# Retention attention and a GELU MLP on one core: q of chunks 3 to 5 transposed by VectorE instead of TensorE, attention given due times, one last copy

## The chip, the cores and the metric

One core of one Trainium2 chip. The metric is the device time of one execution in microseconds (us); of several runs the median is taken. A second number, the span, is that of the profiled execution: from its first to its last instruction. Engines: PE is TensorE (its weight loads are listed apart, as PEld), DVE is VectorE, ACT is ScalarE, POOL is GpSimd, SP only issues DMAs.

## What is computed

A recurrent attention with a decay per head, and behind it a two-layer MLP without biases:

```python
gamma = 1.0 - 2.0 ** (-5.0 - np.arange(H))
scale = 1.0 / np.sqrt(D)
for t in range(S):
    state = gamma[None, :, None, None] * state + np.einsum('bhd,bhe->bhde', k[:, :, t], v[:, :, t])
    y[:, :, t] = scale * np.einsum('bhd,bhde->bhe', q[:, :, t], state)
x = y.transpose(0, 2, 1, 3).reshape(B * S, H * D)
out = gelu_tanh(x @ w_in) @ w_out
```

There are B = 4 batches, H = 8 heads, S = 768 steps and D = 64 columns per head. x is 3072 x 512, w_in 512 x 2048, w_out 2048 x 512. All inputs and the output are float32.

## The kernel before

The sequence is cut into six chunks of 128 steps; a chunk holds all four batches, that is 512 tokens. For each chunk c the kernel does three things.

*Attention.* For each batch, q, k and v (256 KB each, steps on the partitions) are loaded by one DMA each and cast to fp16 (`cast`, L153, L155, L170; q and k of chunks 2 to 5 are cast plainly, v is multiplied by decays in the cast). TensorE transposes q and k of a batch, two heads at a time, into one PSUM bank: `mm_T`, four transposes of 128 x 128 for q and four for k (L205). One copy of 128 x 1024 fp16 moves them to the tile qkT (by DVE, L155, or ACT, L153). `mm_A` (L214) makes the products of k and q inside the chunk; two masked evictions write them to `a` (DVE, L265). `mm_yc` (L233) adds what the state of the earlier chunks gives, `mm_yi` (L245) what the chunk itself gives. DVE evicts the sum with its decay to x (L272), the transposed input of the MLP. `mm_s` (L256) and eight DVE instructions for each half (L277) bring the state up to date. For odd batches the two heads of a pair are swapped in the casts.

*M1.* x @ w_in and GELU. For chunks 2 to 5 it is done as a product of 2 x 2 blocks with 7 multiplications instead of 8 (one Strassen step): 4 groups of 7 units with 4 matmuls each (L486). It needs sums of blocks of x (tile xs, four on POOL), of weights (u_w, t_w) and, behind the GELU, of g (s_g, 16 per chunk, on POOL or DVE, L388). ACT copies the first product of each block from PSUM to a tile st, DVE adds the second (L388), ACT applies the GELU (L367).

*M2.* g @ w_out, also with 7 products: 14 units of 8 matmuls each (L498); ACT copies and DVE adds into the tiles o0 and o1, which SP stores. Chunk 0 and M1 of chunk 1 are done plainly (L351, L509).

The order of the instructions of chunks 1 to 5 is set by a planner that runs while the kernel is built. It has a table KIND with the busy time and latency of each kind of operation on each engine that may do it, and simulates the engines. PE's work is in four threads of units: thread 0 the attention, 1 and 2 M1, 3 M2. Each unit has a due position: M1 of chunk c runs from c to c+1, M2 of chunk c from c+1.15 to c+2.15, the attention of chunk c starts at c-0.9. Of the units that can start now, the attention comes first whatever its position, then the lowest position. Operations of the other engines are chosen by the time at which they can start and then by due time. On each engine the instructions are then issued in this fixed order and wait in it.

Tiles come from pools with a fixed number of slots (SIZE). For raw loads there are ten slots `ld`. SP issues the loads in the order q, k of each batch, then the four v of the chunk; a load is issued when a slot comes free. SP also issues the stores in its one queue.

Of the kernel before, what the change touches and what calls it, by code (L numbers as in the profile page):

```python
# [9 lines left out]
F16 = mybir.dt.float16  # L10
F32 = mybir.dt.float32
# [5 lines left out]
def kernel(  # L17
# [9 lines left out]
    nc = tc.nc  # L27
    B, H, S, Dh = q.shape
    C = 128
    NCk = S // C  # L30
    NHP = H // 2
# [39 lines left out]
    srcs = {"q": q, "k": k, "v": v}  # L71

    SIZE = {
        "ld": (10, [128, H, Dh], F32),
        "qk16": (5, [128, 2, H, Dh], F16),
        "v16": (8, [128, H, Dh], F16),
        "qkT": (5, [128, 2, NHP, 128], F16),
# [6 lines left out]
        "g": (8, [128, 4, B * C], F16),  # L84
    }

    def tile_of(pool, i, shape=None, dt=None):
        n, shape0, dt0 = SIZE[pool]
        return work.tile(shape or shape0, dt or dt0, tag=f"{pool}{i}", name=pool)

    def bank_tile(i, shape=(128, NHP, 128), dt=F32, name="ps"):
        return psum.tile(list(shape), dt, tag=f"b{i}", name=name)

    LD0 = [("st", i) for i in range(6)] + [("ld", i) for i in range(6)]
    LD1 = [("ld", (i + 6) % 10) for i in range(10)] + [("st", 0), ("st", 1)]
    ld_at = {}

    def load1(eng, nm, c, b):
# [100 lines left out]
        BANKS[tag].append(BANKS[tag].pop(0))  # L199
        return bank_tile(BANKS[tag][-1], shape, dt, name)  # L200

    def mm_T(c, b, ps):
        for i, nm in enumerate("qk"):
            for hp in range(NHP):
                nc.tensor.transpose(  # L205
                    out=ps[:, i, hp], in_=pair(h16[nm, c, b], hp), identity=iden
                )
# [395 lines left out]
    for bs in ((0, 1), (2, 3)):  # L603
# [15 lines left out]
        "evS": {"DVE": (1.10, 1.20)},  # L619
        "evT": {"DVE": (0.62, 0.69), "ACT": (0.92, 1.01)},  # L620
        "cast": {"ACT": (0.53, 0.62), "POOL": (0.58, 0.62)},
        "scale": {"POOL": (1.00, 1.05), "DVE": (0.68, 0.75)},
        "scale1": {"POOL": (1.00, 1.05), "DVE": (0.68, 0.75)},
        "sumg": {"POOL": (1.12, 1.16), "DVE": (0.35, 0.42)},
# [25 lines left out]
    def op(*a, **k):  # L650
        todo.append(Op(*a, **k))
# [21 lines left out]
    def take(alloc):  # L673
        for key, readers, *shape in alloc:
            p = key[0]
            i = min((x, i) for i, x in enumerate(slots[p]) if x is not None)[1]
            slots[p][i] = None
            held_by[key] = [p, i, readers, 0.0]
            T[key] = bank_tile(i, *shape) if p == "bank" else tile_of(p, i)
# [9 lines left out]
    def finish_op(o, e, s):  # L689
        busy, lat = KIND[o.kind][e]  # L690
        free_at[e] = s + busy
        end = s + lat + LAT
        if shared(o, e):
            port[0] = s + busy
        if e == "SP":
            begin = max(landed[-1], s + 1.3)
            landed.append(begin + 1.15 * o.kb / 256)
            end = landed[-1] + SAFE
            free_at[e] = max(free_at[e], landed[-4] if o.kind == "load" else 0.0)
        take(o.alloc)  # L700
        o.emit(ENG[e])
        for n in o.early:
            tok[n] = s
        for n in o.gives:
            tok[n] = end
        give_back(o.free, end)


    def cast_in(c, b, nm):
        key = ("v16", c, b) if nm == "v" else ("qk16", c, b)  # L710
        first = nm != "k"

        def emit(eng):
            raw[nm, c, b] = T["ld", nm, c, b]
            h16[nm, c, b] = T[key] if nm == "v" else T[key][:, "qk".index(nm)]
            cast(eng, nm, c, b)

        last = c + 1 == NCk
        kind = "cast" if (nm == "v") == (c < 2) == (nm == "v") and (nm == "v" or c > 1) else "scale"
        if nm == "v":  # L720
            kind = "cast" if c < 2 else "scale"
        elif kind == "scale":
            kind = "scale1"
        op(
            kind, emit,
            [("ld", nm, c, b)] + ([] if first else [("al", key)]),
            [(nm + "16", c, b)],
            alloc=[(key, 1 if last else 2)] if first else [],
            early=[("al", key)] if nm == "q" else [],
            free=[("ld", nm, c, b)],  # L730
            slack=8.0 if nm == "v" else 2.0,
        )

# [1 line left out]

    def load_in(c, b, nm):
        key = ("ld", nm, c, b)

        def emit(eng):
            eng.dma_start(  # L740
                out=T[key], in_=srcs[nm][b, :, c * C:(c + 1) * C, :].rearrange("h p d -> p h d")
            )

        op("load", emit, [prev[0]] if prev[0] else [], [key], alloc=[(key, 1)],
           early=[("issued", key)], slack=3.0, kb=256)
        prev[0] = ("issued", key)

# [3 lines left out]
    def att(c):  # L751
        units = []

        def T1(b):
            def emit():
                mm_T(c, b, T["bank", "T", c, b])

            def ev(eng):
                qkT[c, b] = T["qkT", c, b]
                copy_on(eng, qkT[c, b], T["bank", "T", c, b])  # L760

            op("evT", ev, [("T", c, b)], [("qkT", c, b)], alloc=[(("qkT", c, b), 1)],
               free=[("bank", "T", c, b)], slack=0.5)
            return [sub(0.46, emit, [("q16", c, b), ("k16", c, b)], [("T", c, b)],
                        [(("bank", "T", c, b), 1, (128, 2, NHP, 128), F16)],
                        [("qk16", c, b)])]

        def A(b, cost):
            def emit():
                mm_A(c, b, [T["bank", "A", c, b, j] for j in range(2)])  # L770

            for j in range(2):
                r = j ^ b % 2

                def ev(eng, j=j, r=r):
                    a_sb[c, b, j] = T["a", c, b, j]
                    ev_A1(eng, c, b, j, T["bank", "A", c, b, r])

                op("evA", ev, [("A", c, b)], [("a", c, b, j)], alloc=[(("a", c, b, j), 1)],
                   free=[("bank", "A", c, b, r)], slack=1.0)  # L780
            return sub(cost, emit, [("qkT", c, b)], [("A", c, b)],
                       [(("bank", "A", c, b, j), 1) for j in range(2)])

        def yc(bs):
# [44 lines left out]
        for j in (1, 3, 2, 4) if c > 1 else ():  # L829
            def emit(eng, j=j):  # L830
# [5 lines left out]
            op("sumx", emit, need + ([] if j == 1 else [("al", "xs", c)]), [("xs", c, j)],  # L836
               alloc=[(("xs", c), 1)] if j == 1 else [], early=[("al", "xs", c)] if j == 1 else [],
               slack=0.6)
        return [(c - 0.9 + 0.01 * i, u, True) for i, u in enumerate(units)]

    def m1_raw(c):
        units = []
# [138 lines left out]
    def m2_w(c):  # L981
        units, last = [], c == NCk - 1
        O = [("o0", c), ("o1", c)]
        for n, (k, lk, rk) in enumerate(PROD):
            for a in range(2):
# [41 lines left out]
                if n in SNAP:  # L1027
                    alloc = [(ot, 1 if not last else 9)] if n in (0, 3) and (not last or a == 0) else []

                    def ev(eng, part=part, ot=ot, bank_of=bank_of):  # L1030
                        copy_on(eng, part(T[ot]), bank_of())

                    op("snap", ev, [did] + ([("al", ot)] if last and a else []), [("ev2", c, n, aa)],
                       alloc=alloc, early=[("al", ot)] if alloc else [], free=[key], slack=0.0)
                elif n in ADD:
                    def ev(eng, part=part, ot=ot, bank_of=bank_of):
                        tt(eng, part(T[ot]), bank_of(), part(T[ot]), ALU.add)

                    op("add", ev, [did, ("ev2", c, SNAP_OF[at], aa)], [("ev2", c, n, aa)],
                       free=[key], slack=0.0)  # L1040
                elif not (last and a == 1):
                    def ev(eng, part=part, ot=ot, bank_of=bank_of):
                        copy_on(eng, part(T[ot]), bank_of())

                    op("snap", ev, [did], [("ev2", c, n, aa)], free=[key], slack=0.2)
                else:
                    def ev(eng, ot=ot, key=key):
                        t, p = T[ot][:, 1], T[key]
                        nc.vector.tensor_copy(out=t[:, 0:hw // 2], in_=p[:, 0:hw // 2])  # L1049
                        nc.scalar.copy(out=t[:, hw // 2:hw], in_=p[:, hw // 2:hw])  # L1050

                    op("snap", ev, [did], [("ev2", c, n, aa)], free=[key], slack=0.2)
                if not last and n > 4:
# [47 lines left out]

    for c in range(1, NCk):
        if c > 1:
            for b in range(B):
                load_in(c, b, "q")
                load_in(c, b, "k")
            for b in range(B):
                load_in(c, b, "v")
        for b in range(B):
            for nm in "qkv":  # L1110
                cast_in(c, b, nm)
# [49 lines left out]
    while waiting or any(threads):  # L1161
        best = {}
        fronts, held_off = [], False
        for i, th in enumerate(threads):
# [4 lines left out]
                continue  # L1169
            s = max(need, free_at["PE"], r if r is not None else 1e9)  # L1170
            fronts.append([s, i, th[0], need, r])
        if fronts and fronts[0][1] == 0:
            s, _, _, need, r = fronts[0]
            if need < free_at["PE"] + 0.5 and s > max(need, free_at["PE"]):
                held_off = True
# [22 lines left out]
        if e == "PE":  # L1198
            sure = min(h[5] for h in fronts)
            ok = [h for h in fronts if h[5] <= sure + 0.03]  # L1200
            h = min(ok, key=lambda h: (h[1] != 0, h[2][0]))
            start_unit(threads[h[1]].pop(0), h[0])
        else:
            ok = [x for x in cand[e] if x[0] <= best[e] + 0.02]
            s, _, o = min(ok, key=lambda x: x[1])
            waiting.remove(o)
            finish_op(o, e, s)
# [30 lines left out]
```

## Time and profile before

| what | value |
|---|---|
| median of the runs | 207.44 us (207.22 to 208.33) |
| profiled execution, its own time | 207.19 us |
| its span | 205.3 us, so 1.9 us lie around it |
| TensorE clock granted | 1.0 throughout |
| HBM read, written | 27.64 MB, 6.29 MB |
| queue of SP (q1) | 72256 packets, 23.45 MB, 45.6% of the span of 16 DMA engines |
| chain that ended last | PE 39%, of it L498 21%, L486 15%, L205 1% |

How to read it: busy times are sums over an engine's instructions, merged where they overlap. In the chain of work that ended last, PE's part is followed back only to 120.7 us, where PE last waited for nothing. A mean duration of a pipelined instruction is longer than the distance from one start to the next; where many of one kind stand in a row, the timeline gives that distance. A wait names the engine that waited, its line, and what released it.

### The profile page before, as it was taken

What the parts mean: (1) busy time and instruction counts of PE and PEld (TensorE: products, weight loads), DVE (VectorE), ACT (ScalarE), POOL (GpSimd) and SP (SyncE); (2) the same over time, 40 slices, a digit from 0 to 9 for tenths busy, and PEclk for the clock granted to TensorE, in tenths of its full rate; (3) what the DMA queues carried; (4) which work ended last, traced back from release to release, by engine and by line L of the source; (5) the groups of instructions that cost most, each with busy time, mean ns of one, the idle gap of its engine ahead of it and who ended that gap; (6) DMA issues with size and microseconds to landing.
All of it is one profiled execution on the core that took longest, in us unless ns stands there. A gap on an engine that the chain in (4) does not pass through costs nothing. (4 is left out here: it accounts for less than half of the span.)

```text
span 205.3 us, 5809 instructions
## 1 busy us (share of the span) xinstructions
PE 196.2 (96%) x2424; PEld 156.6 (76%) x2424; DVE 147.6 (72%) x284; ACT 124.4 (61%) x223; POOL 87.8 (43%) x90
## 2 busy tenths in 40 slices
PE   7869999999999998999999999999999999999993
PEld 2346744455898887788888879888888888888882
DVE  3335585749868999997998899989656864476421
ACT  2482466054689566476599749965856577765311
POOL 0587000030222973936999957982441520024000
PEclk9999999999999999999999999999999999999999
DMA  7999999999998998976799500023000140002204
GB/s 165 287 260 206 209 204 220 219 224 240 247 209 258 255 217 194 264 173 140 231 220 249 126 3 3 0 83 129 0 0 3 42 158 8 0 5 102 102 29 179
DMA packets 83034, 30.11 MB, mean 147 GB/s; under 512 B 75456, under 2 KB 79936, under 8 KB 83008
## 3 DMA queue, kind: packets, MB, share of 16 engines
q1 hardware_dynamic: 72256, 23.45, 45.6%
q0 software_dynamic: 4224, 4.19, 12.3%
q10 hardware_dynamic: 6528, 2.10, 4.1%
q8 instruction: 19, 0.31, 0.6%
q14 instruction: 7, 0.06, 0.1%
HBM read 27.64 MB, written 6.29 MB: 165 GB/s over the span
## 5 line engine op out<-in xcount | busy, mean ns | idle before, releaser
L388 DVE TENSOR_TENSOR st<-ps,st 128x512 f32<-128x512 f32 x48 | 31.7, 683 | 10.1 <-PE ps L486 8.9
L367 ACT ACTIVATE g<-st 128x512 f16<-128x512 f32 x48 | 29.4, 633 | 14.4 <-DVE st L388 14.0
L153 ACT COPY st<-ps 128x512 f32<-128x512 f32 x48 | 27.2, 590 | 11.6 <-PE ps L486 11.4
L498 PEld LDWEIGHTS <-s_g 128*128 128x128 f16 x320 | 31.1, 98 | 3.6
L486 PEld LDWEIGHTS <-w_in 128*128 128x128 f16 x256 | 24.7, 98 | 3.7 <-issue 0.6
L388 POOL TENSOR_TENSOR s_g<-g 128x512 f16<-128x512 f16 x12 | 14.0, 1177 | 30.5 <-ACT st L153 23.4
L351 PEld LDWEIGHTS <-w_in 128*128 128x128 f16 x232 | 20.9, 98 | 7.7 <-issue 0.7
L265 DVE TENSOR_TENSOR a<-ps,mask 128x512 f16<-128x512 f32 x40 | 24.8, 679 | 2.5 <-PE ps L214 2.4
L498 PEld LDWEIGHTS <-g 128*128 128x128 f16 x240 | 23.3, 98 | 2.8
L153 ACT COPY o<-ps 128x512 f32<-128x512 f32 (+1 forms) x27 | 14.3, 528 | 17.7 <-PE ps L498 13.4
L367 ACT ACTIVATE g<-ps 128x512 f16<-128x512 f32 x32 | 19.1, 602 | 7.7 <-PE ps L351 5.2
L486 PEld LDWEIGHTS <-u_w 128*128 128x128 f16 x192 | 18.4, 98 | 2.4
L498 PE MATMUL ps<-w_out,s_g 128*128 128x256 f16 x160 | 19.9, 273 | 0.0
L498 PE MATMUL ps<-t_w,s_g 128*128 128x256 f16 x160 | 19.8, 273 | 0.0
L498 PE MATMUL ps<-w_out,g 128*128 128x256 f16 x160 | 19.8, 273 | 0.0
L388 POOL TENSOR_TENSOR s_g<-g,s_g 128x512 f16<-128x512 f16 x13 | 15.3, 1193 | 10.1 <-ACT g L367 3.9
L486 PE MATMUL ps<-xs,w_in 128*128 128x256 f16 x128 | 19.1, 273 | 0.0
L388 DVE TENSOR_TENSOR s_g<-g 128x512 f16<-128x512 f16 x28 | 14.6, 562 | 6.0 <-ACT g L367 3.6
L388 DVE TENSOR_TENSOR o<-ps,o 128x512 f32<-128x512 f32 (+1 forms) x18 | 10.8, 598 | 11.0 <-PE ps L498 10.9
L486 PE MATMUL ps<-x,w_in 128*128 128x256 f16 x128 | 18.1, 272 | 0.3 <-DVE a L265 0.3
L486 PE MATMUL ps<-xs,u_w 128*128 128x256 f16 x128 | 17.8, 273 | 0.0
L153 ACT COPY qkT<-ps 128x1024 f16<-128x1024 f16 x11 | 11.1, 1018 | 8.2 <-PE ps L205 8.0
(71 smaller groups left out, 319.7 us busy)
## 6 DMA issues: line engine op xcount, KB each, us to landing
ld<-in_k_dram SPq DMA_DIRECT2D x21, 256.0 KB, 4.5
ld<-in_q_dram SPq DMA_DIRECT2D x21, 256.0 KB, 4.4
ld<-in_v_dram SPq DMA_DIRECT2D x19, 256.0 KB, 4.4
out_dram<-o SPq DMA_DIRECT2D x8, 512.0 KB, 2.7
w_in<-in_moe_w_in_dram POOLq DMA_DIRECT2D x4, 512.0 KB, 9.7
w_out<-in_moe_w_out_dram POOLq DMA_DIRECT2D x4, 512.0 KB, 14.7
out_dram<-o SPq DMA_DIRECT2D x5, 256.0 KB, 3.6
st<-in_v_dram SPq DMA_DIRECT2D x3, 256.0 KB, 4.6
```

Of the source, the lines that this page charges most:

```text
L153: eng.copy(out=out, in_=in_)
L265: eng.tensor_tensor(out=a_sb[c, b, j], in0=ps, in1=mask[:, j], op=ALU.mult)
L351: nc.tensor.matmul(out=out, lhsT=w_in_sb[wi][:, kc, wr * 128:(wr + 1) * 128], rhs=xT[c][:, kc, t0:t1], start=(kc == 0), stop=(kc == NHP - ...
L367: nc.scalar.activation(out=out, in_=in_, func=AF.Gelu_apprx_tanh, scale=1.0)
L388: eng.tensor_tensor(out=out, in0=in0, in1=in1, op=op)
L486: nc.tensor.matmul(out=ps[:, f], lhsT=m1_lhs(lk, kc, 2 * g + f), rhs=x[:, kc], start=(n in FIRST and kc == 0 and f == 0), stop=(n in (1, 5 ...
L498: nc.tensor.matmul(out=ps, lhsT=m2_lhs(c, lk, fp, a), rhs=m2_rhs(rk, fp), start=(first and fp == 0), stop=(n in (1, 5, 6) and fp == NP - 1 ...
```

## The change

q of chunks 3 to 5 takes another way.

- Its load is one operation of the planner for a whole chunk: 16 DMAs on SP, each 32 partitions wide with runs of 32 floats (128 B), which place q so that a transposition inside blocks of 32 x 32 gives the layout of qkT. They write one new tile `ldq` (4 slots `lq`), which the loads of chunk 1 and the first four of chunk 2 use as well; the pool `ld` shrinks from ten slots to six.
- The cast stays, on ACT or POOL; for batches 1 and 3 it is two copies, each of 64 partitions, which swap the two halves.
- DVE transposes the cast tile in blocks of 32 x 32 straight into the q half of qkT, 128 x 512 in one instruction.
- TensorE transposes k alone (four transposes), and its eviction has 128 x 512.
- The attention pieces get positions from c-0.7 to c-0.2, spread evenly, so inside M1 of the chunk before, and the planner takes the lowest position, with no precedence for attention.
- The copy of the very last product, in two halves on DVE and ACT before, is one operation, which the planner's table gives to ACT.

```diff
-        "ld": (10, [128, H, Dh], F32),
+        "ld": (6, [128, H, Dh], F32),
+        "lq": (4, [128, H, Dh], F32),
...
+    BLK = (3, 4, 5)
+    ldq = const.tile([128, B, 4 * 128], F32, name="ldq")
...
-    LD1 = [("ld", (i + 6) % 10) for i in range(10)] + [("st", 0), ("st", 1)]
+    LD1 = [("lq", i) for i in range(4)] + [("ld", i) for i in range(6)] + [("st", 0), ("st", 1)]
...
-    def mm_T(c, b, ps):
-        for i, nm in enumerate("qk"):
+    def mm_T(c, b, ps, nms="qk"):
+        for i, nm in enumerate(nms):
...
+        "cast2": {"ACT": (1.06, 1.15), "POOL": (1.18, 1.22)},
+        "trq": {"DVE": (0.60, 0.69)},
+        "evTk": {"DVE": (0.36, 0.44), "ACT": (0.50, 0.58)},
+        "loadq": {"SP": (8.6, 0.0)},
...
-            landed.append(begin + 1.15 * o.kb / 256)
+            landed.append(max(begin + 1.15 * o.kb / 256, s + busy + 1.8 if o.kind == "loadq" else 0.0))
...
+    def q_cast(c, b):
+        key = ("qk16", c, b)
+
+        def emit(eng):
+            o = T[key][:, 0].rearrange("p h d -> p (h d)")
+            if b % 2 == 0:
+                copy_on(eng, o, ldq[:, b])
+            else:
+                copy_on(eng, o[0:64], ldq[64:128, b])
+                copy_on(eng, o[64:128], ldq[0:64, b])
...
+        def tr(eng):
+            qkT[c, b] = T["qkT", c, b]
+            eng.transpose(
+                out=qkT[c, b][:, 0].rearrange("p hp t -> p (hp t)"),
+                in_=T[key][:, 0].rearrange("p h d -> p (h d)"),
+            )
...
+    def q_load(c):
+        src = q.rearrange("b (hp j) s (dd d) -> j dd s (b hp) d", j=2, dd=2)
+        t = ldq.rearrange("p b (hp a d) -> p (b hp) a d", a=4, d=32)
+
+        def emit(eng):
+            for j in range(2):
+                for dd in range(2):
+                    for a in range(4):
+                        p0, t0 = (2 * j + dd) * 32, c * C + a * 32
+                        eng.dma_start(out=t[p0:p0 + 32, :, a, :], in_=src[j, dd, t0:t0 + 32])
...
+            if c in BLK:
+                def emit():
+                    mm_T(c, b, T["bank", "T", c, b], "k")
+
+                def ev(eng):
+                    copy_on(eng, T["qkT", c, b][:, 1], T["bank", "T", c, b][:, 0])
...
-        return [(c - 0.9 + 0.01 * i, u, True) for i, u in enumerate(units)]
+        return [(c - 1 + 0.3 + 0.5 * i / len(units), u, True) for i, u in enumerate(units)]
...
-                        t, p = T[ot][:, 1], T[key]
-                        nc.vector.tensor_copy(out=t[:, 0:hw // 2], in_=p[:, 0:hw // 2])
-                        nc.scalar.copy(out=t[:, hw // 2:hw], in_=p[:, hw // 2:hw])
+                        copy_on(eng, T[ot][:, 1, 0:hw], T[key])
...
-        if fronts and fronts[0][1] == 0:
+        if fronts and fronts[0][1] == 0 and fronts[0][2][0] <= min(h[2][0] for h in fronts):
...
-            h = min(ok, key=lambda h: (h[1] != 0, h[2][0]))
+            h = min(ok, key=lambda h: h[2][0])
```

More of the change, by code (lines that the diff above doesn't have):

```diff
@@ L85 @@
     }
+    BLK = (3, 4, 5)
+    ldq = const.tile([128, B, 4 * 128], F32, name="ldq")
     def tile_of(pool, i, shape=None, dt=None):
         n, shape0, dt0 = SIZE[pool]
+        if pool == "lq":
+            return ldq[:, i].rearrange("p (h d) -> p h d", h=H)
         return work.tile(shape or shape0, dt or dt0, tag=f"{pool}{i}", name=pool)
@@ L676, in take @@
             i = min((x, i) for i, x in enumerate(slots[p]) if x is not None)[1]
+            if p == "lq" and key[2] in BLK:
+                i = key[3]
             slots[p][i] = None
@@ L706, in finish_op, with ld_key @@
         give_back(o.free, end)
+    def ld_key(c, b, nm):
+        early = c == 2 and b < 2 and nm != "v" or c in BLK and nm == "q"
+        return ("lq" if early else "ld", nm, c, b)
+    def q_cast(c, b):
[7 more added lines that the diff above has]
+                copy_on(eng, o[64:128], ldq[0:64, b])
+        op("cast2" if b % 2 else "cast", emit, [("ld", "q", c)], [("q16", c, b)],
+           alloc=[(key, 2 if c + 1 == NCk else 3)], early=[("al", key)], free=[("lq", "q", c, b)], slack=2.0)
+        def tr(eng):
[4 more added lines that the diff above has]
+            )
+        op("trq", tr, [("q16", c, b)], [("qT", c, b)], alloc=[(("qkT", c, b), 1)],
+           early=[("al", "qkT", c, b)], free=[key], slack=1.5)
+    def q_load(c):
[7 more added lines that the diff above has]
+                        eng.dma_start(out=t[p0:p0 + 32, :, a, :], in_=src[j, dd, t0:t0 + 32])
+        key = ("ld", "q", c)
+        op("loadq", emit, [prev[0]], [key], alloc=[(("lq", "q", c, b), 1) for b in range(B)],
+           early=[("issued", key)], slack=3.0, kb=1024)
+        prev[0] = ("issued", key)
     def cast_in(c, b, nm):
+        if c in BLK and nm == "q":
+            return q_cast(c, b)
         key = ("v16", c, b) if nm == "v" else ("qk16", c, b)
         first = nm != "k"
+        ldk = ld_key(c, b, nm) if c > 1 else ("ld", nm, c, b)
         def emit(eng):
-            raw[nm, c, b] = T["ld", nm, c, b]
+            raw[nm, c, b] = T[ldk]
             h16[nm, c, b] = T[key] if nm == "v" else T[key][:, "qk".index(nm)]
@@ L729, in cast_in @@
             early=[("al", key)] if nm == "q" else [],
-            free=[("ld", nm, c, b)],
+            free=[ldk],
             slack=8.0 if nm == "v" else 2.0,
@@ L737, in load_in @@
         key = ("ld", nm, c, b)
+        ldk = ld_key(c, b, nm)
         def emit(eng):
             eng.dma_start(
-                out=T[key], in_=srcs[nm][b, :, c * C:(c + 1) * C, :].rearrange("h p d -> p h d")
+                out=T[ldk], in_=srcs[nm][b, :, c * C:(c + 1) * C, :].rearrange("h p d -> p h d")
             )
-        op("load", emit, [prev[0]] if prev[0] else [], [key], alloc=[(key, 1)],
+        op("load", emit, [prev[0]] if prev[0] else [], [key], alloc=[(ldk, 1)],
            early=[("issued", key)], slack=3.0, kb=256)
@@ L756, in emit @@
                 mm_T(c, b, T["bank", "T", c, b])
+            if c in BLK:
[3 more added lines that the diff above has]
+                    copy_on(eng, T["qkT", c, b][:, 1], T["bank", "T", c, b][:, 0])
+                op("evTk", ev, [("T", c, b), ("al", "qkT", c, b)], [("kT", c, b)],
+                   free=[("bank", "T", c, b)], slack=0.5)
+                return [sub(0.24, emit, [("k16", c, b)], [("T", c, b)],
+                            [(("bank", "T", c, b), 1, (128, 1, NHP, 128), F16)],
+                            [("qk16", c, b)])]
             def ev(eng):
@@ L780, in A @@
                    free=[("bank", "A", c, b, r)], slack=1.0)
-            return sub(cost, emit, [("qkT", c, b)], [("A", c, b)],
+            got = [("qT", c, b), ("kT", c, b)] if c in BLK else [("qkT", c, b)]
+            return sub(cost, emit, got, [("A", c, b)],
                        [(("bank", "A", c, b, j), 1) for j in range(2)])
@@ L1103 @@
         if c > 1:
+            if c in BLK:
+                q_load(c)
             for b in range(B):
-                load_in(c, b, "q")
+                if c not in BLK:
+                    load_in(c, b, "q")
                 load_in(c, b, "k")
```

## The prediction

> **What bounds the kernel now.** I read the busy line of the page first, then the table of stretches, then PE's waits, then the timelines of PE and of SP's queue.
>
> ```profile
> span 205.3 us, 5809 instructions
> PE 196.2 (96%) x2424; PEld 156.6 (76%) x2424; DVE 147.6 (72%) x284; ACT 124.4 (61%) x223; POOL 87.8 (43%) x90
> ```
>
> PE is busy for 96% of the span. The table of stretches says where the other 9.1 us lie (columns: stretch, its length, busy us of PE, PEld, DVE, ACT, POOL with instruction counts, granted clock, DMA share, GB/s):
>
> ```profile
> 40.00:75.00 35.00, 34.89 (x516) 27.05 (x515) 26.97 (x52) 22.01 (x37) 11.95 (x13) 1.00 0.98 235
> 75.00:110.00 35.00, 34.33 (x541) 29.57 (x540) 33.71 (x63) 24.17 (x45) 26.54 (x28) 1.00 0.89 211
> 110.00:145.00 35.00, 34.71 (x533) 29.90 (x531) 33.15 (x59) 26.04 (x45) 25.18 (x23) 1.00 0.26 71
> 145.00:201.80 56.80, 56.78 (x521) 50.65 (x518) 31.62 (x61) 33.41 (x65) 12.55 (x11) 1.00 0.13 48
> ```
>
> From 40 to 201.8 us PE is idle for 161.80 - 160.71 = 1.09 us in all; the rest is start-up and the tail, which the change hardly touches. So a PE instruction taken out of the middle is time taken off the end, as long as the others keep feeding PE. The same rows name the engine to fear: DVE is busy for 66.9 of the 70 us from 75 to 145, then for only 31.6 of 56.8. PE's waits from 45 to 202 us are short and are mostly for DVE (columns: us in total, times, longest):
>
> ```profile
> PE ps L245 <- DVE v L170: 0.4, 1, 0.4
> PE ps L486 <- DVE a L265: 0.3, 1, 0.3
> PE ps L205 <- DVE o L388: 0.2, 1, 0.2
> ```
>
> **PE loses 48 transposes.** `mm_T` (L205) issues 8 per chunk and batch, four for q and four for k; 3 chunks x 4 batches x 4 = 48 go. Their price is the distance of starts in PE's timeline, not the 219 ns of one, since they are pipelined:
>
> ```profile
> 108.77 1.06 PE L205 MATMUL ps<-iden,qk 128*128 128x128 f16 x16
> 109.66 0.60 PE L486 MATMUL ps<-xs,u_w 128*128 128x256 f16 x4
> ```
>
> 16 take 109.66 - 108.77 = 0.89 us, so one takes 56 ns and 48 take **2.67 us**. All lie on the path, as PE idles only 1.09 us there.
>
> The Trainium skill, VectorE: DVE Perf Modes, section The three transpose paths, prices one TensorE transpose of 128x128 at 390 ns and the VectorE one at 311 ns, and its rules for kernel authors keep 128x128 transposes on TensorE where PSUM will do. By its 390 ns the 48 would be worth 18.7 us; the pitch of 56 ns in this stream decides.
>
> **DVE gains 12 block transposes** (fp16, 128x512, SBUF to SBUF); the trace has none. Nearest rows on DVE with 512 columns: the fp16 sums at 0.41 us when alone, and L265 at 0.61 us from start to start (2.47 us for four), 0.68 us for one. I take 0.6, one column per cycle as in L265: 7.2 us, bounds 4.9 to 8.2. Against that, the evictions of the transposes halve. From 75 to 145 us the qkT copies of 1024 columns are 5 on DVE (3.39 us) and 7 on ACT (7.03 us); with 512 columns I take half and a little more, 0.38 and 0.55 each, which saves DVE 1.5 us and ACT 3.2. Net DVE +5.7 us (bounds +3 to +7).
>
> **Casts.** For batches 1 and 3 the q cast becomes two copies of 64 partitions, 6 more instructions. At 0.62 us (ACT) or 0.61 (POOL) for a whole cast, they cost 1.8 (half each) to 3.7 us, on engines busy for 50.2 and 51.7 of the 70 us. No cost on the path.
>
> **Where DVE's 5.7 us go.** In the old place they would exceed the 3.1 us that DVE has free from 75 to 145. But the attention moves too. Today it goes first whenever it is ready: chunk 5's transposes start at 125.5, and by then 181 of the 448 matmuls of L486 have run, that is 69 of chunk 3's 112; its last piece ends at 144.4, with 21 of chunk 4's 112 done. The new due times put it from 30% to 73% of chunk 4's M1, later by about half an M1. Chunk 4's start (102.8, at 79% of chunk 2's M1) moves likewise; chunk 3 (14% to 79% of chunk 2's M1) stays and is drawn together. So part of the DVE work of attention slides behind 145 us, where DVE has 25 us free. PE fills the place with M1 and M2 that is waiting: 204 L486 and 209 L498 matmuls run from 144.4 to 189.5. What is late next is x of the next chunk: four sums on POOL of 1.16 us each must follow the last eviction, 4.6 us inside the last quarter of an M1. For PE's idle time I therefore take **no change**; bounds -1.1 (all the idle goes) to +2.6 (the 5.7 us of DVE less its 3.1 free, nothing slid). I take zero because both engines that could pay for it have room after 145.
>
> **Loads.** One q load of a chunk is 16 DMAs of 64 KB with 8192 packets of 128 B, in place of 4 of 256 KB with 4096 packets. On SP's queue:
>
> ```profile
> 99.98 0.41 SPq L740 DMA_DIRECT2D ld<-in_q_dram  x1
> 102.03 0.38 SPq L740 DMA_DIRECT2D ld<-in_k_dram  x1
> ...
> 109.02 4.50 SPq L740 DMA_DIRECT2D ld<-in_v_dram  x4
> ```
>
> An issue takes 0.37 us at least and 0.87 at the median, when the queue is full; 16 take 5.9 to 13.9 us, against 3.5 for four at the median. The planner allows 8.6. Behind them on SP wait the k and v loads and the stores of o. The load also waits for all four q casts of the chunk before, as its buffer is one tile. What hides it: with attention spread, a chunk's load has about an M1 and an M2 to land, over 20 us. The DMA share falls to 0.26 after 110, so bytes do not bind. On the path I take 0, bounds 0 to 5.3 us (13.9 - 8.6).
>
> **Last copy.** Today the halves run one after the other, though on two engines:
>
> ```profile
> 200.95 0.37 ACT L153 COPY o<-ps 128x256 f32<-128x256 f32 x1 [4.00 <-PE ps L498]
> ...
> 201.82 0.29 DVE L1049 COPY o<-ps 128x128 f32<-128x128 f32 x1 [1.32 <-PE ps L498]
> 202.15 0.27 ACT L1050 COPY o<-ps 128x128 f32<-128x128 f32 x1 [0.83 <-DVE o L1049]
> ```
>
> From 201.82 to 202.42 is 0.60 us; one copy of 256 columns is the row above, 0.37. **-0.23 us**, all at the end, as only the last store follows.
>
> **Sum.** The profiled execution took 207.19 us (span 205.3 and 1.9 around it). 207.19 - 2.67 - 0.23 + 0 = 204.3. The median of the runs shown, 207.44, is 0.25 above the profiled run, so 204.5 for a median.
>
> **Rivals.**
>
> A, *the spread also removes idle time*. For it: the waits above are for DVE where it is saturated. Then up to 1.1 us more goes: 203.4. Against it: any new order has waits of its own.
>
> B, *DVE takes the transposes' place*. The 12 transposes stand between a q cast and the A matmuls, on the engine that was 96% busy. If the attention's DVE work does not slide, 2.6 us of it cannot be absorbed, POOL being two to three times as slow on a sum (1.16 against 0.41): 204.5 + 2.6 = 207.1, no change that can be told. Against it: the 25 us free behind 145.
>
> C, *late q loads stall the queues, slower*. Place: the casts of k in chunks 4 and 5, whose loads stand behind the 16 q issues on SP. If an issue takes 0.87 us, the loads land 5.3 us later than the planner thinks; a cast on ACT or POOL then holds the gelus and evictions behind it, and PE stops soon after. It decides when an issue takes over 0.54 us (8.6/16) and the plan has left less than the difference as slack. Price: 5.3 us in one chunk, 204.5 + 5.3 = 209.8; more if two. For it: the plan trusts its table, and POOL already waited 5.7 us for a q load in this trace (chunk 2, the start of the prefetch). Against it: the issues of 64 KB have half the packets of those measured, and the chunks' loads are far ahead of use (chunk 5's were issued by 113.5 and first cast at 124.4).
>
> The Trainium skill, DMA: Bandwidth & Descriptors, section Bandwidth, measures 0.95 us for a 64 KB transfer issued from GpSimd and calls transfers below 64 KB dominated by descriptors; 16 of them in a row would be an estimated 15.2 us, which speaks for C. No transfer of this trace has that shape.
>
> D, *the due times hurt*: x of the next chunk comes too late for M1, because only the last quarter of an M1 is left for two evictions and four sums. PE then lives on M2; where that is not ready it waits 1 to 2 us per chunk, three times: 204.5 + 3 to 6 = 207.5 to 210.5. I count half with B, half with C.
>
> **Numbers.** 0.5% is about what a measurement of this kernel can tell from no change, so faster means below 206.4 and slower above 208.5. Forecast (203.7 to 206.4) 0.58; A 0.12; B with half of D 0.14; C with half of D 0.16. Faster 0.70, same 0.14, slower 0.16. The range reaches to A's end and to the upper edge of the same: 203.0 to 208.5; outside lies mostly C.
>
> **What would show it.** Right: 144 L205 matmuls instead of 192; DVE with 12 transposes near 0.6 us; PE's idle time from 40 us to its last matmul about 1.1 us; attention of chunk 5 starting well behind 125 us; one copy of 0.37 us behind the last matmul. For B: PE waits on qkT or a from DVE, DVE near 100% past 145. For C: ACT or POOL waiting on DMA for qk, SP issues over 0.54 us. For D: PE waiting on xs from POOL. The prediction fails if PE's idle time in the middle grows by over 2 us.

## The result and the profile after

The changed kernel takes **204.52 us** (median of 4 runs, 204.46 to 204.77); the kernel before, beside it, 207.33 (206.84 to 208.33). The ratio is 0.987, with a 95% interval of 0.9841 to 0.9898: faster by 1.0 to 1.6%. Runs more than 1.5% above the fastest of the same kernel are left out of all medians and ratios here, which concerns two of e9's ten. The forecast was 204.5. The total is right, and the experiments show that one of the terms behind it is not.

The head of the page, and the table of stretches with the same columns as before:

```profile
span 202.7 us, 5761 instructions
...
PE 192.5 (95%) x2376; PEld 153.1 (76%) x2376; DVE 150.5 (74%) x283; ACT 126.6 (62%) x235; POOL 96.6 (48%) x96
```

```profile
40.00:75.00 35.00, 34.89 (x518) 27.08 (x517) 27.22 (x52) 21.42 (x36) 10.89 (x11) 1.00 0.90 200
75.00:110.00 35.00, 33.65 (x491) 29.06 (x490) 31.64 (x62) 24.84 (x47) 25.91 (x27) 1.00 0.82 186
110.00:145.00 35.00, 34.12 (x474) 29.54 (x472) 32.74 (x56) 27.66 (x53) 23.64 (x23) 1.00 0.59 129
145.00:199.00 54.00, 54.00 (x574) 47.77 (x573) 36.57 (x64) 33.65 (x67) 24.47 (x21) 1.00 0.12 47
```

PE has 48 instructions fewer and 3.7 us less busy time. But between 40 us and its last matmul it is now idle for 159.00 - 156.66 = 2.34 us, where it was 1.09. Nearly all of it (2.23 us) lies between 75 and 145 us, though DVE is less busy there than before (64.4 us of the 70, from 66.9). PE's waits from 40 us on name the places:

```profile
PE ps L504 <- ACT o L159: 0.7, 1, 0.7
PE ps L504 <- DVE s_g L394: 0.5, 1, 0.5
PE ps L492 <- DVE a L271: 0.5, 1, 0.5
PE ps L492 <- DVE st L394: 0.4, 1, 0.4
```

The three waits of the kernel before are gone; four others stand in their place. So the change takes more from PE than it gives to the end, and something gives part of it back. To follow that through all runs I use two numbers worked out from the starts of PE's matmuls in each trace. **The middle** is the time from the first plain matmul of M2 (at 34 us) to the start of the last matmul. **The stalls** are the sum, inside the middle, of the gaps between starts beyond the usual distance (216, 109, 56 and 28 ns for 512, 256, 128 and 64 columns), of those over 0.1 us.

| us | before | after | difference | forecast |
|---|---|---|---|---|
| 48 transposes of 56 ns | | | -2.67 | -2.67 |
| PE's stalls | 2.71 | 3.67 | +0.96 | 0 |
| the middle, which holds both | 167.13 | 165.32 | -1.81 | -2.67 |
| start of the last copy to the end of the span | 3.48 | 3.01 | -0.47 | -0.23 |
| start of the middle | 34.38 | 34.09 | -0.29 | 0 |
| the profiled execution | 207.19 | 204.52 | -2.67 | -2.9 |

The start of the middle lies between 33.66 and 34.70 us in all traces but one, so its -0.29 is scatter. (The one is e13's: 35.46 us, with a granted clock of 0.66 from 15 to 20 us.) The tail's gain is larger than forecast; e3 below shows how much of it is the copy. The main question for the experiments is the +0.96: whether the new due times, the new path of q, or neither makes the stalls.

### The profile page after: what moved, and what is told of

Same layout as the page of the kernel before. It is cut to its first block, busy times and chain, and to the rows that moved or that the text cites. A ratio compares the mean times of both kernels' runs of the same rounds, so it can differ in the third digit from the quotient of the medians.

```text
span 202.7 us, 5761 instructions
## 1 busy us (share of the span) xinstructions
PE 192.5 (95%) x2376; PEld 153.1 (76%) x2376; DVE 150.5 (74%) x283; ACT 126.6 (62%) x235; POOL 96.6 (48%) x96
## 5 line engine op out<-in xcount | busy, mean ns | idle before, releaser
L159 ACT COPY st<-ps 128x512 f32<-128x512 f32 x48 | 26.4, 602 | 13.0 <-PE ps L492 12.8
L373 ACT ACTIVATE g<-st 128x512 f16<-128x512 f32 x48 | 29.9, 649 | 7.3 <-DVE st L394 7.3
L394 POOL TENSOR_TENSOR s_g<-g 128x512 f16<-128x512 f16 x17 | 19.9, 1184 | 13.9 <-ACT g L373 13.9
L394 POOL TENSOR_TENSOR s_g<-g,s_g 128x512 f16<-128x512 f16 x15 | 17.8, 1191 | 16.2 <-DVE s_g L394 16.1
L159 ACT COPY o<-ps 128x512 f32<-128x512 f32 (+1 forms) x28 | 14.8, 529 | 17.0 <-PE ps L504 14.1
L504 PE MATMUL ps<-t_w,s_g 128*128 128x256 f16 x160 | 18.9, 273 | 1.2 <-ACT o L159 0.7
L504 PE MATMUL ps<-w_out,g 128*128 128x256 f16 x160 | 19.3, 273 | 0.0
L394 POOL TENSOR_TENSOR s_g<-s_g,g 128x512 f16<-128x512 f16 x10 | 11.9, 1187 | 14.8 <-DVE s_g L394 14.7
L492 PE MATMUL ps<-xs,u_w 128*128 128x256 f16 x128 | 16.6, 273 | 0.5 <-DVE a L271 0.5
L492 PE MATMUL ps<-x,w_in 128*128 128x256 f16 x128 | 16.3, 273 | 0.0
L357 PE MATMUL ps<-x,w_in 128*128 128x256 f16 x128 | 15.3, 273 | 0.1
```

What stands on the lines that cost most here:

```text
L159: eng.copy(out=out, in_=in_)
L357: nc.tensor.matmul(out=out, lhsT=w_in_sb[wi][:, kc, wr * 128:(wr + 1) * 128], rhs=xT[c][:, kc, t0:t1], start=(kc == 0), stop=(kc == NHP - ...
L373: nc.scalar.activation(out=out, in_=in_, func=AF.Gelu_apprx_tanh, scale=1.0)
L394: eng.tensor_tensor(out=out, in0=in0, in1=in1, op=op)
L492: nc.tensor.matmul(out=ps[:, f], lhsT=m1_lhs(lk, kc, 2 * g + f), rhs=x[:, kc], start=(n in FIRST and kc == 0 and f == 0), stop=(n in (1, 5 ...
L504: nc.tensor.matmul(out=ps, lhsT=m2_lhs(c, lk, fp, a), rhs=m2_rhs(rk, fp), start=(first and fp == 0), stop=(n in (1, 5, 6) and fp == NP - 1 ...
```

## The experiments

My theory behind the forecast was that both halves of the change act as one: due times slide DVE's work to where it has room, so that PE's lost transposes are all gained. The rivals were those of the prediction: the due times alone bring a gain (A), DVE takes the transposes' place (B), the loads or the due times bring new waits (C, D). All kernels compute the whole result; two of them repeat work for nothing, as told there. The runs were made beside the kernel before, with medians of 207.01 to 207.14 for it.

### e1: the new path of q with the old due times

```diff
-        return [(c - 1 + 0.3 + 0.5 * i / len(units), u, True) for i, u in enumerate(units)]
+        return [(c - 0.9 + 0.01 * i, u, True) for i, u in enumerate(units)]
...
-        if fronts and fronts[0][1] == 0 and fronts[0][2][0] <= min(h[2][0] for h in fronts):
+        if fronts and fronts[0][1] == 0:
...
-            h = min(ok, key=lambda h: h[2][0])
+            h = min(ok, key=lambda h: (h[1] != 0, h[2][0]))
```

> The changed kernel with the old due positions of attention (from c-0.9) and its old precedence; q of chunks 3 to 5 still goes over DVE. Theory (PE's work sets the time; the due times only have to keep PE fed while DVE has 5.7 us more): attention bunches again, DVE has 3.1 us free from 75 to 145 us and gets 5.7 more, so PE's idle time from 40 us on grows by up to 2.6 us: 205.5 to 207.1 us. Rival 1 (the due times alone brought the gain, the transposes nothing): 207.3. Rival 2 (the due times brought nothing): 204.5.

### e2: the new due times with the old path (the kernel before, the same three places the other way)

> The kernel before with the new due positions and the choice by lowest position, nothing else; 192 transposes on PE. Theory: PE's work is that of before, so 207.3 us less at most its idle time of 1.1 us: 206.2 to 207.6. Rival 1 (the due times alone brought the gain): 204.5 to 205. If new waits come with the new order whatever the transposes do, it is above 207.6.

Measured, with the two known kernels as the other corners:

| median, us (ratio, interval) | old due times | new due times |
|---|---|---|
| old path of q | 207.14 (before) | e2: 205.77 (0.9925, 0.9900 to 0.9950) |
| new path, one last copy | e1: 209.54 (1.0110, 1.0065 to 1.0155) | after: 204.52 (0.9870, 0.9841 to 0.9898) |

With the old due times the new path of q makes the kernel *slower* by 2.4 us, though PE has 2.67 us less to do. The stalls are 8.67 us there. Its longest waits of PE, and the stretch they lie in:

```profile
PE ps L492 <- DVE st L394: 2.4, 2, 1.9
PE ps L492 <- DVE a L271: 1.3, 1, 1.3
```

```profile
110.00:145.00 35.00, 30.79 (x487) 25.69 (x486) 33.27 (x55) 23.49 (x45) 29.48 (x28) 1.00 0.51 116
```

DVE is at 33.27 us of 35 and PE loses 4.21 us in this stretch alone: that fits rival B, DVE in the transposes' place. Late loads (rival C) don't explain it: from 75 to 150 us one wait for a load stands in this trace, 1.2 us of POOL before 120.5, and PE's longest wait had ended at 115.7. The due times alone gain 1.37 us without one transpose less (stalls 1.63, from 2.71): that is rival A. Its stretches show PE without idle time where DVE has room:

```profile
75.00:110.00 35.00, 34.33 (x508) 29.96 (x507) 33.47 (x64) 24.20 (x47) 28.03 (x26) 1.00 0.76 185
110.00:145.00 35.00, 35.00 (x498) 30.84 (x496) 27.26 (x49) 26.12 (x49) 26.54 (x25) 1.00 0.35 91
```

From 110 to 145 us DVE's busy time is 27.26, against 33.15 in the kernel before: the slide of attention that the prediction worked out, 5.9 us of DVE. So A holds, and the new path of q brings new stalls, as B had it. Of the change's 2.6 us by medians the due times bring 1.37, and the new path with the last copy another 1.25.

### e3: the last copy in two halves again

```diff
-                        copy_on(eng, T[ot][:, 1, 0:hw], T[key])
+                        t, p = T[ot][:, 1], T[key]
+                        nc.vector.tensor_copy(out=t[:, 0:hw // 2], in_=p[:, 0:hw // 2])
+                        nc.scalar.copy(out=t[:, hw // 2:hw], in_=p[:, hw // 2:hw])
```

> The changed kernel with the last copy in two halves again, on DVE and ACT. Theory (the halves run one after the other, 0.60 us against 0.37): 204.5 + 0.23 = 204.75 us. If the whole shorter tail of the changed kernel (0.5 us from PE's last matmul to the end) is due to the copy: 205.0. If the halves ran side by side: 204.4.

204.91 us (204.47 to 206.51, 10 runs), ratio 0.9901 (0.9874 to 0.9929). The copy is worth 0.39 us by the medians, with intervals that overlap. The traces are sharper. In after the one copy takes 0.37 us, where the two halves of before took 0.60 from the start of the first to the end of the second (0.59 in e3):

```profile
199.72 0.37 ACT L159 COPY o<-ps 128x256 f32<-128x256 f32 x1 [0.50 <-PE ps L504]
```

So the copy gives the 0.23 us of the forecast. The rest of the tail lies behind the copy and doesn't go with it: from the end of the last copy to the end of the span it is 2.89 us in before and 2.63 in e3, both with halves, and 2.64 in after and 2.89 in e7, both with one copy. (In e15 it is 3.49.) That part of the tail's -0.47 is scatter. The profiled execution of e3 is the longest of its ten runs, so its waits are not used.

### e4: 48 transposes back on PE, nothing else moved

The four transposes of k are issued twice in chunks 3 to 5; the second set writes the same bank with the same values, and the plan of all engines stays.

```diff
             if c in BLK:
                 def emit():
                     mm_T(c, b, T["bank", "T", c, b], "k")
+                    mm_T(c, b, T["bank", "T", c, b], "k")
```

> The changed kernel with PE's 48 transposes put back without a use: in chunks 3 to 5 the four transposes of k are issued twice into the same bank. Plan, loads, DVE and all else as in the changed kernel. Theory (PE is the bound, 56 ns each): 204.5 + 2.67 = 207.2 us, less what falls into PE's idle time of 2.3 us, so 206.5 to 207.2. Rival 1 (PE's work does not count, the gain is the order's): 204.5 to 205.

206.64 us (206.02 to 208.25, 10 runs), ratio 0.9984 (0.9955 to 1.0013): +2.12 against after, with intervals apart. In the trace the middle grows by 1.95 us, to 167.27, while the stalls shrink by 0.64, to 3.03: 2.67 - 0.64 = 2.03. So a transpose taken from PE is worth its 56 ns to the end, less what a stall next to it swallows. This term of the sum holds.

### e10: each block transpose of DVE twice

```diff
-            eng.transpose(
-                out=qkT[c, b][:, 0].rearrange("p hp t -> p (hp t)"),
-                in_=T[key][:, 0].rearrange("p h d -> p (h d)"),
-            )
+            for _ in range(2):
+                eng.transpose(
+                    out=qkT[c, b][:, 0].rearrange("p hp t -> p (hp t)"),
+                    in_=T[key][:, 0].rearrange("p h d -> p (h d)"),
+                )
```

> The changed kernel with each of DVE's 12 block transposes issued twice; plan, PE and loads unchanged. Question: the due times alone gave 205.8 us, and PE has 2.67 us less to do in the changed kernel, but it gained only 1.25 more; are the 2.0 us of new waits of PE due to DVE's added work? Theory 1 (they are): 7.3 us more on DVE bring about as many waits again, 206 to 208. Rival (DVE's load is not it; the waits come from the order that the plan took): DVE has slack, 204.5 to 205.

208.17 us (207.95 to 208.30, 4 runs), ratio 1.0054 (1.0036 to 1.0072): +3.65 us for 12 more instructions at 0.61, 7.3 us of DVE. Half of what is added to DVE reaches the end. PE's stalls are 7.36 us, and the longest waits are for DVE:

```profile
PE ps L492 <- DVE a L271: 1.0, 2, 0.7
PE ps L220 <- DVE qkT L742: 0.8, 1, 0.8
```

DVE is thus still a second bound: what is put on it costs about 0.5 us each us, even with the new due times. No run has the new loads and the smaller pool `ld` without DVE's transposes, so their share in the stalls of after isn't shown.

### e7 and e12: which chunks

The path for two chunks, `BLK = (4, 5)` (e7), and for one, `BLK = (3,)` (e12); both are replanned.

```diff
-    BLK = (3, 4, 5)
+    BLK = (4, 5)
```

> The changed kernel with only chunks 4 and 5 on the new path, 16 fewer transposes saved. If PE's saving of 0.89 us per chunk counts and the waits come in equal shares, the time lies on the line from 205.5 (none, due times and one copy) to 204.5 (three): 204.9. If chunk 3, the one with the least slack, brings most of the new waits: 204.0 to 204.4.

> The changed kernel with chunk 3 alone on the new path. Chunks 4 and 5 alone gave 203.6 us with 1.6 us of PE stalls over 0.1 us, all three 204.5 with 3.7. Theory 3 (it is chunk 3 on the new path that brings the waits, at 74 to 78 us, where four sums on DVE run 3.3 us beside POOL and DVE's transpose and ACT's q cast come in between): stalls of 2.3 us or more with the group at 74 to 78 us, and 0.89 saved against none (205.8 less 0.4 for the copy): 204.9 to 205.6. Rival (the waits come from having three chunks, whichever): stalls of 1.6, 204.2 to 204.6.

| kernel | median, us | ratio (interval) | the middle | stalls |
|---|---|---|---|---|
| e2, no chunk | 205.77 | 0.9925 (0.9900 to 0.9950) | 165.98 | 1.63 |
| e12, chunk 3 | 205.67 | 0.9938 (0.9915 to 0.9962) | 166.25 | 2.92 |
| e7, chunks 4 and 5 | 203.59 | 0.9841 (0.9823 to 0.9859) | 164.19 | 1.63 |
| after, chunks 3 to 5 | 204.52 | 0.9870 (0.9841 to 0.9898) | 165.32 | 3.67 |

Chunks 4 and 5 give their full price: 32 transposes of 56 ns are 1.78 us, and 165.98 - 1.78 = 164.20, measured 164.19, with no stall more. Chunk 3 gives nothing: its 0.89 us of transposes comes with 1.29 us of stalls. PE's longest waits in e12 are the first two of after, word for word, and e7 has neither:

```profile
PE ps L504 <- ACT o L159: 0.7, 1, 0.7
PE ps L504 <- DVE s_g L394: 0.5, 1, 0.5
```

They stand at 79 and 80 us. After has two more stalls, at 118 and 132 us, of 1.21 us together; neither e7 (0.0 us from 110 to 145) nor e12 (0.1) has them, so here they come only with all three chunks. Where the first two come from can be followed in the timelines of after. PE first (start, us, what, and the idle time before it with its releaser):

```profile
79.38 0.60 PE L504 MATMUL ps<-t_w,s_g 128*128 128x256 f16 x4 [0.70 <-ACT o L159]
80.51 1.70 PE L504 MATMUL ps<-t_w,s_g 128*128 128x256 f16 x14 [0.53 <-DVE s_g L394]
```

ACT, whose copy of `o` PE waits for:

```profile
76.36 0.63 ACT L373 ACTIVATE g<-st 128x512 f16<-128x512 f32 x1 [1.53 <-DVE st L394]
76.90 0.57 ACT L159 COPY st<-ps 128x512 f32<-128x512 f32 x1
78.22 0.63 ACT L373 ACTIVATE g<-st 128x512 f16<-128x512 f32 x1 [0.76 <-DVE st L394]
78.76 0.57 ACT L159 COPY o<-ps 128x512 f32<-128x512 f32 x1
```

And DVE, whose `st` ACT waits for:

```profile
73.06 2.67 DVE L394 TENSOR_TENSOR s_g<-g 128x512 f16<-128x512 f16 x2
75.65 0.68 DVE L394 TENSOR_TENSOR st<-ps,st 128x512 f32<-128x512 f32 x1
76.25 0.69 DVE L741 STREAM_TRANSPOSE qkT<-qk 128x512 f16<-128x512 f16 x1
77.50 0.69 DVE L394 TENSOR_TENSOR st<-ps,st 128x512 f32<-128x512 f32 x1 [0.55 <-ACT st L159]
```

Read upwards: PE's slot for a product of M2 comes free when ACT has copied `o`, from 78.76 to 79.33. ACT issues in its fixed order, and ahead of that copy stand two GELUs, which wait 1.53 and 0.76 us for DVE's sums `st`. The first of these is late because two fp16 sums of g took 2.67 us on DVE, 1.3 each, where such a sum alone took 0.41; DVE's new transpose comes behind them, and DVE is idle for 0.55 us after it. In e7 the plan has a copy of `o` in front of the GELUs. They wait as long there, but PE doesn't wait for ACT:

```profile
74.37 0.59 ACT L159 COPY o<-ps 128x512 f32<-128x512 f32 x1 [0.25 <-ACT qk L159]
...
76.32 0.63 ACT L373 ACTIVATE g<-st 128x512 f16<-128x512 f32 x1 [0.88 <-DVE st L394]
78.55 0.63 ACT L373 ACTIVATE g<-st 128x512 f16<-128x512 f32 x1 [1.61 <-DVE st L394]
```

That these waits come with chunk 3's new path, as this planner orders it, is shown by e7 and e12; in e9 below the same path is planned with other costs, and they are gone. The chain through ACT's order is read from these rows; no run moved that one copy alone.

### e9 and e11: does the plan misjudge DVE?

A part of the chain is DVE's time beside POOL. The planner's table has 0.68 us for a scaling of v on DVE and 0.35 for a sum of g; in after they take 1.04 us (mean of 9) and 0.54 to 0.61. The medians are 0.68 and 0.42: most run at their usual length, and a few take up to 1.64 and 1.38. The Trainium skill, SBUF — State Buffer, section Who interferes with whom, says that a DVE instruction with two inputs in SBUF contends with a GpSimd instruction that reads SBUF. The rows agree: three scalings of v took 4.18 us while POOL was in sums and a scaling.

```profile
113.14 4.18 DVE L176 TENSOR_TENSOR v<-ld,cst 128x512 f16<-128x512 f32 x3
117.25 2.47 DVE L271 TENSOR_TENSOR a<-ps,mask 128x512 f16<-128x512 f32 x4
```

Behind them stand the masked evictions to `a`, and for these PE waited 0.47 us until 117.98, the third wait of the list.

e9 tells the planner the measured costs; e11 takes v's scaling off DVE altogether.

```diff
-        "scale": {"POOL": (1.00, 1.05), "DVE": (0.68, 0.75)},
+        "scale": {"POOL": (1.10, 1.15), "DVE": (1.00, 1.07)},
...
-        "sumg": {"POOL": (1.12, 1.16), "DVE": (0.35, 0.42)},
+        "sumg": {"POOL": (1.12, 1.16), "DVE": (0.55, 0.62)},
```

> The changed kernel with other costs in the planner's table, near what the trace shows beside a busy POOL: v's scaling on DVE 1.00 instead of 0.68 (trace 1.04), on POOL 1.10 (trace 1.22), the sums of g on DVE 0.55 instead of 0.35 (trace 0.54 to 0.61). No instruction changes in kind, only place and engine. Theory 2 (PE's waits stem from DVE instructions that the plan takes for shorter than they are): stalls of PE over 0.1 us fall from 3.7 us to 1.5 to 2.5, time 202.8 to 204. Rival (the waits are DVE's load itself): 204.3 to 205.5.

```diff
-        "scale": {"POOL": (1.00, 1.05), "DVE": (0.68, 0.75)},
+        "scale": {"POOL": (1.10, 1.15)},
```

> The changed kernel with v's scaling of chunks 2 to 5 on POOL alone (16 instead of 7 there, 9 fewer on DVE, 9.1 us less for DVE). Theory 1 (DVE's load makes the waits): clearly faster, 202.5 to 204. Theory 2 (too short costs in the plan): the long v scalings on DVE are gone, the sums stay too short: 203.5 to 204.5. Rival (POOL becomes late, it gets 11 us more): 205 or more.

e9: 204.85 us (median of eight runs, 203.37 to 205.87; the other two took 207.75 and 209.73), ratio 0.9890 (0.9856 to 0.9923). The waits at 79 us are gone, but the stalls are 4.00 us in all, and the runs scatter more than those of any other kernel here. The theory that the too short costs are *the* cause of the stalls finds no support; a plan with the mean costs was not a better plan.

e11: **203.43 us** (203.22 to 204.87, 4 runs), ratio 0.9848 (0.9804 to 0.9892). Stalls 2.43, from 3.67. The waits for `a` and `st` past 110 us are gone and PE is busy for the whole of that stretch; those at 79 us stay:

```profile
PE ps L504 <- DVE s_g L394: 0.8, 1, 0.8
PE ps L504 <- ACT o L159: 0.7, 1, 0.7
```

So about a third of the stalls of after (1.24 us) goes with v's scaling off DVE. For half of that, the 0.63 us stall at 118, the rows above show the scalings in front of the evictions that PE waited for. For the other half, at 132, they don't: no scaling of v stands on DVE from 118 to 131 us, and DVE itself waited 1.42 us for ACT there. The kernel is planned anew here too, so other instructions have moved with it.

### e13, e14 and e15: an earlier chunk, and both improvements at once

e13 puts chunk 2 on the new path and leaves chunk 3 on the old one, e14 joins e7 and e11, e15 joins e13 and e11.

```diff
-    BLK = (3, 4, 5)
+    BLK = (2, 4, 5)
...
-        early = c == 2 and b < 2 and nm != "v" or c in BLK and nm == "q"
+        early = c in BLK and nm == "q"
...
-        op("loadq", emit, [prev[0]], [key], alloc=[(("lq", "q", c, b), 1) for b in range(B)],
+        op("loadq", emit, [prev[0]] if prev[0] else [], [key], alloc=[(("lq", "q", c, b), 1) for b in range(B)],
```

> The changed kernel with chunks 2, 4 and 5 on the new path and chunk 3 on the old one (the load of chunk 2's q uses ldq, its k no longer). PE does as little as in the changed kernel. Theory 3: DVE has room before 75 us (27 of 35 busy), so 0.89 less than with chunks 4 and 5: 202.7, up to 203.3 with small new waits. Rival (each added chunk brings its own waits): 203.6 to 204.8. A late load of chunk 2, whose q must wait for all four first casts of chunk 1, would show as waits of ACT or POOL on DMA before 60 us.

> The changed kernel with chunks 4 and 5 on the new path and v's scaling on POOL alone. The one wait of PE for v on DVE near 78 us (0.5 us) should go: 203.1. If POOL's added work makes other waits: 203.6 or more.

> Both: chunks 2, 4 and 5 on the new path, v on POOL alone. By addition 202.2 to 202.8; 203.6 or more if the two get in each other's way.

| kernel | median, us | ratio (interval) | the middle | stalls |
|---|---|---|---|---|
| e13, chunks 2, 4, 5 | 206.38 | 0.9974 (0.9953 to 0.9995) | 166.50 | 4.45 |
| e14, chunks 4, 5 and v on POOL | 204.62 | 0.9872 (0.9833 to 0.9911) | 164.56 | 2.03 |
| e15, chunks 2, 4, 5 and v on POOL | 212.58 | 1.0264 (1.0247 to 1.0281) | 172.02 | 9.74 |

None of them beats e7 or e11. e13 shows the first half of rival C's mechanism, a load that an engine stands still for, far more strongly than after (e15 shows the same): SP issues chunk 2's q from 47.5 to 58.1 us, with the loads of k behind it, and POOL, with casts of that q at the head of its order, stands still (SP's and POOL's timelines and a wait of ACT in e13):

```profile
47.53 10.57 SPq L758 DMA_DIRECT2D ldq<-in_q_dram  x16
58.20 4.09 SPq L800 DMA_DIRECT2D ld<-in_k_dram  x4
```

```profile
60.88 2.58 POOL L161 CAST qk<-ldq 64x512 f16<-64x512 f32 x4 [15.52 <-DMA ld<-in_k_dram]
```

```profile
ACT qk L159 <- DMA ldq<-in_q_dram: 0.5, 1, 0.5
```

The casts read `ldq`, so what POOL waited for is the load of q, as in ACT's wait for it, though POOL's row names k.

PE did not wait for it: in e13 it is idle for 0.11 us from 40 to 75, as in after. Of e13's 4.45 us of stalls, 4.18 stand behind 75 us (1.57 to 110, 1.20 to 145, 1.41 later), and its longest waits are mostly for DVE. So the late load itself cost PE nothing; why the plan with chunk 2 waits more later on isn't shown. In e15 POOL has all of v's scaling, and PE waited 1.3 us for its sums xs: that is rival D's mechanism, which no other kernel here shows. e14's two gains don't add (stalls 2.03, between those of e7 and e11). As each of these kernels is a new plan, that can't be laid to one instruction. The two best versions are e7 (203.59) and e11 (203.43), with middles of 164.19 and 164.20 us. They beat both kernels by the medians; their intervals overlap that of after and each other's, so which of the two is better stays open.

## Why the prediction came out right

**What bounds the kernel: right.** PE is busy for 95% of the span, and e4 shows that a transpose on it goes to the end at nearly its full 56 ns.

**48 transposes, -2.67: right** (144 of L211 are left; e4: +2.03 by stalls and price, +2.12 by medians).

**PE's idle time, no change: wrong as a step**, inside its bounds of -1.1 to +2.6. By the starts it grew by 0.96, by the busy rows by 1.25. It is a sum of two terms that the prediction had listed as rivals and given 0.12 and (B with half of D) 0.14: the due times take 1.08 us of stalls away (before to e2, rival A), and the path of q puts 2.04 there (e2 to after, rival B). I took zero "because both engines that could pay for it have room after 145". DVE does have it, and work did slide, but the waits come before 145, at single places where an instruction stands in a fixed order behind a late one. Room in another stretch doesn't help them. B's own signs came only in part: PE waited for `a` from DVE once (0.5 us) and never for qkT, and past 145 us DVE is at 68%, not near 100%. What DVE's load does is shown by e10 and e1; that a wait falls at just these places is the plan's order.

**DVE's work: the instruction right, the balance off.** The transposes were not in the trace before; they are now:

```profile
L741 DVE STREAM_TRANSPOSE qkT<-qk 128x512 f16<-128x512 f16 x12 | 8.1, 689 | 0.3 <-ACT qk L159 0.3
L159 ACT COPY qkT<-ps 128x512 f16<-128x512 f16 x12 | 6.9, 591 | 0.0
```

689 ns each, and 0.60 to 0.63 from start to start in a row, as taken. The halved evictions did not cost 0.38 on DVE: all 12 went to ACT, at 0.59 where I took 0.55. DVE's busy time grew by 2.9 us, not 5.7, because the planner also answered: 10 of the 80 sums of g moved from DVE to POOL (48 to 38 on DVE), whose busy time grew by 8.8. The prediction treated a fixed load; a planner moves it. Nor did the total decide: DVE was less busy from 75 to 145 us than before, and PE's stalls there grew from 2.45 to 3.30 us.

**Casts, no cost: right, with another price.** A cast of 64 partitions takes as long as one of 128, so the upper of the two prices holds:

```profile
L159 ACT CAST qk<-ldq 64x512 f16<-64x512 f32 x10 | 6.2, 617 | 4.6 <-PE ps L262 4.5
L159 ACT CAST qk<-ldq 128x512 f16<-128x512 f32 x4 | 2.5, 622 | 0.6 <-DMA out_dram<-o 0.6
```

**Loads, 0 on the path: right, with no margin.** SP's queue took for the 16 issues of chunks 3, 4 and 5:

```profile
61.99 9.83 SPq L758 DMA_DIRECT2D ldq<-in_q_dram  x16
...
83.58 9.83 SPq L758 DMA_DIRECT2D ldq<-in_q_dram  x16
...
111.78 10.21 SPq L758 DMA_DIRECT2D ldq<-in_q_dram  x16
```

That is 0.61 us each, above the 0.54 that the prediction named as rival C's condition, and 1.2 to 1.6 more than the plan's 8.6. For chunk 3 the last of them was issued at 71.3 and landed some 2.8 us later, at about 74.1; the first cast, on ACT at 74.21, had stood 0.56 us. So the slack was used up, and both halves of C's condition were met by a little. It cost nothing, since ACT then stood another 1.53 us for DVE's sum. In e13 POOL stood for 15.5 us and PE still did not wait: the prediction's step from a late cast to a stopped PE was too quick.

**Rival D** did not appear in after: no wait of PE for xs (it did in e15). Chunk 5's attention moved from 125.5 to 139.5 as foreseen.

**Last copy, -0.23: right** by the rows (0.37 in place of 0.60). The tail shrank by 0.47, and the other 0.24 is scatter behind the copy.

So the total was hit in part by luck: 0.96 us of stalls that I had at zero stand against 0.24 of scatter in the tail, 0.29 at the start, and some 0.2 of smaller remainders. That leaves the profiled execution, 204.52, 0.2 us above its forecast of 204.3. The forecast of 204.5 for a median held 0.25 us more, which before's runs had shown and after's don't (its median is its profiled time); that hid the rest. With the old due times the same -2.67 and -0.23 would have missed by 5 us, as e1 shows.

## What to carry to other kernels

Where one engine is at 95% and the next at 90% in the same stretch, price work moved between them by both: here an us taken from PE was worth 0.8 to 1 us where no new wait came with it (e4, e7) and nothing where one did (e12), and an us put on DVE cost about half of one. Test a change of order apart from the change of work it comes with; the order alone was worth 1.4 us with the old work and 5.0 with the new. An "idle time unchanged" should be written as its two terms, what goes and what comes, since an average of busy time over a stretch says nothing of the single instruction that is late in a fixed order.

## What the hardware showed unexpectedly

- Half the partitions don't halve an instruction: 617 ns for 64 x 512, 622 for 128 x 512 (casts on ACT, above).
- DVE's instructions with two SBUF inputs stretch beside POOL by more than the plan's table has: v's scaling 1.39 us in the row of three and a sum of g 1.3 in the row of two, against 0.68 and 0.41 at their shortest. Most are not stretched (medians 0.68 and 0.42), so a mean price fits neither kind.
- In e15, after PE had been busy for only 2.74 us of 5, its granted clock (the column before the last two) fell to 0.53 in the next 5 us, though it was then busy throughout:

```profile
110.00:115.00 5.00, 2.74 (x44) 1.90 (x44) 5.00 (x8) 2.63 (x5) 5.00 (x6) 0.79 0.81 127
115.00:120.00 5.00, 5.00 (x27) 3.47 (x25) 2.21 (x3) 2.97 (x5) 4.61 (x5) 0.53 0.71 124
```

16 matmuls of 256 columns took from 114.04 to 117.40 there, 0.21 each, twice the usual 0.109. So a stall of PE can cost more than its length. From 114.04 to 119.85, 28 matmuls of 256 columns took 5.8 us, where 28 x 0.109 is 3.05; the 2.75 us more are part of e15's stalls of 9.74 and of its 212.58 us. The Trainium skill, TensorE: Matmul & The Clock Gate, Part 1, says that the array falls to half its clock after an idle window of about 3.4 us and needs as much steady work to come back. The drop to half agrees. What the trace shows before it is no idle window of that length, but waits of 0.2 to 1.3 us between short groups of matmuls, and the usual pitch came back only after some 5.7 us of steady work. In e10, with PE busy for 32.08 us of the 35 from 75 to 110, the clock stayed at 1.00.
